# A long-convolution layer with a relu MLP on one core: the product stage regrouped by four frequencies, with a shifted tile for one of its results

## Chip, core, metric

One core of one Trainium2 chip runs the whole program. The metric is device microseconds (us) of one execution. Three executions of the kernel before took 213.0, 213.03 and 213.28 us, so the median is 213.03 us. All other times come from one further execution that was recorded by the hardware profiler: it took 213.07 us in all, of which 211.2 us are the span from the first recorded instruction to the last.

The engines are TensorE (PE for its matmuls, PEld for its weight loads), VectorE (DVE), ScalarE (ACT), GpSimd (POOL) and SyncE (SP, which only issues DMAs). L425 means line 425 of the kernel before.

## What is computed

Input x, k and v are 2048 tokens of 512 channels. The reference, cut to what matters:

```python
k_shift = short causal convolution of k over 4 tokens
kv   = k_shift * v
y    = irfft(rfft(kv padded to 4096) * rfft(ssm_k padded to 4096))[:2048]
h    = x + layernorm(x) * (y + kv * ssm_D)
out  = h + relu(layernorm(h) @ w1) @ w2          # w1 is 512 x 1376, w2 is 1376 x 512
```

The transform, the product and the inverse transform are done as matmuls with tables of sines, in 4-byte floats.

## The kernel before, in words

**Stages.** (1) Up to about 51 us: loads, sine tables, the short convolution (`taps`, L333), transposes of its input (`to_rows`, L278) and the first half of the forward transform (`stage1`, L294) of the filter into the tile BK and of the data into the tile BX. (2) 51.1 to 91.1 us: **the product stage** (L418 to L455), the second half of both forward transforms, frequency index k1 = 0 to 31, and the product of filter and data. (3) 91.1 to 114.2 us: the first half of the inverse transform (`inv1`, L541), 16 blocks. (4) to the end: the second half of the inverse (`inv2`, L634), the gate, and the MLP.

**The product stage.** BK and BX have the places [2 parts i][32 g][32][8] in each of 128 partitions. For one k1, `cols` takes the g of one parity, k1 % 2, and there the two places 2v and 2v+1 with v = k1 // 2: the data of k1 = 2v and of k1 = 2v+1 lie in the same two places, one in the even g and the other in the odd g. Two kinds of unit work on them; each unit has a PSUM buffer of two banks and runs an x = 0 part on BK and then an x = 1 part on BX:

- `pairs(k1)` (tile u, L425): 8 matmuls of 64 rows by 256 columns, which run two at a time, one on the upper and one on the lower 64 rows of the array. That makes 4 steps of two matmuls each: parts i = 0 and i = 1 on BK, then i = 0 and i = 1 on BX. Its product is written in place into `BK[:, :, :, k1, :]`, that is, into place k1 of every g, odd and even.
- `sums(k1)` (tile us, L435): 8 matmuls of 128 rows by 256 columns, for k1 and k1 + 1, with weights from the table tile smc. Its product is written in place into `BX[:, 0, :, k1:k1+2, :]`.

A step below is the start-to-start time of such matmuls. `times` (L439) then finishes a unit: ACT copies the BK half of the PSUM buffer to SBUF (`forms`, L415, tiles ktu and kts with two buffers each), and DVE multiplies it with the other half and writes the product (L442).

The order is written out by hand: for every two k1 the loop (L445) issues the matmuls of `sums(k1)`, `pairs(k1)`, `pairs(k1 + 1)`, and then `times` of the three. ACT and DVE take units in that same order. For k1 = 0 all x = 0 parts come first. The pool psF has four buffers of two banks, so a unit may start only when the product of the fourth unit before it has been read out by DVE. The semaphore waits follow from the order of issue and from what overlaps: a product waits for all matmuls issued before it that read the places it overwrites.

`sum_tables(c)` (L376) lets POOL write the weights for the sums of four k1 into one of four places of smc; the first four groups are made before the stage, the others follow as places come free. `add_chunks` (L406, POOL) prepares column sums of w1, which `column_means` (L460, tile pm) needs right after the stage.

**After it.** `inv1_mm` (L535) makes one output of 256 columns from three accumulated matmuls: part 0 on the sums' products (`BX[:, 0]`, with inv3), parts 1 and 2 on the two halves of the pairs' products (BK, with inv12). All three are 256 columns wide; in parts 1 and 2 half of the 256 columns of the table are zeros. `inv1_begin` starts part 0 of blocks 0 and 1. Everything contracts over all k1, so no inverse matmul can run before the last products that it reads are written.

Of the kernel before, what the change touches and what calls it, by code (L numbers as in the profile page):

```python
# [10 lines left out]
BF16 = mybir.dt.bfloat16  # L11
F32 = mybir.dt.float32
F32R = mybir.dt.float32r
I32 = mybir.dt.int32
PSUM = bass.MemoryType.PSUM
P = 128
# [40 lines left out]
def kernel(  # L57
# [13 lines left out]
    nc = tc.nc  # L71
# [5 lines left out]
    DC = D // P  # L77
    NFC = (DFF + P - 1) // P
    x_d, k_d, v_d, out_d = A_q[0], A_k[0], A_v[0], out[0]
    lo, hi = slice(0, 64), slice(64, 128)  # L80
    halves = (lo, hi)

    pl = _Pools(tc)
    ctx.enter_context(tc.manual_schedule())
    consts = pl.push("consts")
    bkp = pl.push("bkp")
    bxp = pl.push("bxp")
    c0p = pl.push("c0p")
    stp = pl.push("stp")
    skp = pl.push("skp")  # L90
    early = pl.push("early")
    xkp = pl.push("xkp", side="right")
    psum = pl.push("psF", bufs=4, space=PSUM)

    BK = bkp.tile([P, 2, 32, 32, DC * 2], F32R, tag="K", name="BK")
    E = bxp.tile([P, 16384], F32, tag="X", name="E")
    F = xkp.tile([P, 4096], F32, tag="F", name="F")
    G = skp.tile([P, 4096], I32, tag="G", name="G")  # L100
    taken = [15424]

    def view(at, n, dt, t=E):
# [22 lines left out]
    for dp in range(2):  # L126
        src = bass.AP(tensor=A_ssm_D.tensor, offset=A_ssm_D.offset, ap=[[0, 1], [1, DC * P]])
        nc.scalar.dma_start(out=draw[64 * dp:64 * dp + 1, :], in_=src)
    zero = consts.tile([P, 512], BF16, name="zero")
    nc.vector.memset(zero[:], 0.0)  # L130
    nc.vector.memset(kT[0][:, :, 0:16], 0.0)
    for c in range(4):
# [20 lines left out]
    def fill(ps, n):  # L153

        for _ in range(n):
            nc.tensor.matmul(out=ps, lhsT=zero[:, 0:P], rhs=zero[:], start=True, stop=True, skip_group_check=True)

    fill(bank2("psz")[:, 0, :], 22)

# [46 lines left out]
    dpm = small([2, 64], F32)  # L206
# [10 lines left out]
    st = stp.tile([P, 32, 192], F32R, name="st")  # L217
# [12 lines left out]
    for dp in range(2):  # L230
        row = slice(64 * dp, 64 * dp + 1)
        for rp in range(2):
            for sp in range(2):
                src = draw[row, 256 * rp:256 * rp + 256].rearrange("p (r u s l d) -> p r u s l d", r=2, s=2, l=2, d=2)[:, :, :, sp, :, dp]
# [8 lines left out]
    esc = consts.tile([P, DC], F32, name="esc")  # L243
    ebi = consts.tile([P, DC], F32, name="ebi")
    core0 = c0p.tile([P, 32, P], F32R, name="core0")
    ecore = [core0[:].rearrange("p (h i r) x -> p h i r x", h=2, i=4)] + [None] * 3
    ecw = {0: tsn.rearrange("p a b -> p (a b)")[:, 0:1024].rearrange("p (h x) -> p h x", h=2)}

    def ec_turns(q):
# [9 lines left out]

    def ec_sins(q, rs=range(DC)):  # L260
        for r in rs:
            nc.scalar.activation(out=ecore[q][:, :, :, r, :], in_=ecw[q].rearrange("p h (i x) -> p h i x", i=4),  # L262
                                 func=ACT.Sin, scale=esc[:, r:r + 1], bias=ebi[:, r:r + 1])

    def copy(eng, o, i):
# [72 lines left out]


    inv3 = consts.tile([P, 2, 2, 64], F32R, name="inv3")  # L340
    inv12 = consts.tile([P, 6, 64], F32R, name="inv12")
    ones = consts.tile([P, P], F32R, name="ones")
    for gb in range(7):
        if gb == 6:
# [13 lines left out]
            taps(gb // 2, gb % 2)  # L358

    nc.gpsimd.memset(inv3[:].bitcast(F32), 0.0)  # L360
    nc.gpsimd.memset(inv12[:].bitcast(F32), 0.0)
    nc.gpsimd.tensor_tensor(out=dpm[:, 0, :], in0=dsc[:, 0, :], in1=dsc[:, 1, :], op=ALU.add)
    nc.gpsimd.tensor_tensor(out=dpm[:, 1, :], in0=dsc[:, 1, :], in1=dsc[:, 0, :], op=ALU.subtract)
    for dst, pq, src, sgn in ((inv12[lo, 2, :], lo, dpm[lo, 0, :], 1.0), (inv12[lo, 3, :], lo, dpm[lo, 1, :], 1.0),
                              (inv12[hi, 2, :], hi, dpm[hi, 1, :], 1.0), (inv12[hi, 3, :], hi, dpm[hi, 0, :], -1.0),
                              (inv3[lo, 0, 0, :], lo, dsc[lo, 1, :], -1.0), (inv3[lo, 0, 1, :], lo, dsc[lo, 0, :], 1.0),
                              (inv3[hi, 1, 0, :], hi, dsc[hi, 1, :], -1.0), (inv3[hi, 1, 1, :], hi, dsc[hi, 0, :], 1.0)):
        nc.gpsimd.tensor_single_scalar(out=dst, in_=src, scalar=sgn / 2048, op=ALU.mult)
    nc.gpsimd.memset(ones[:].bitcast(F32), 1.0 / D)


    smc = skp.tile([P, 4, 2, 4, P], F32R, tag="G", name="smc")
    for dp, pq in enumerate(halves):
        nc.gpsimd.memset(smc[pq, :, :, :, 64 - 64 * dp:128 - 64 * dp].bitcast(F32), 0.0)

    def sum_tables(c):  # L376
        ks = slice(4 * c, 4 * c + 4)
        for dp, pq in enumerate(halves):
            for i, op in ((0, ALU.subtract), (1, ALU.add)):
                nc.gpsimd.tensor_tensor(out=smc[pq, c % 4, i, :, 64 * dp:64 * dp + 64], in0=st[pq, ks, 64:128].bitcast(F32),  # L380
                                        in1=st[pq, ks, 0:64].bitcast(F32), op=op)

    for c in range(4):
        sum_tables(c)

    xfl = xkp.tile([P, P, 64], BF16, tag="F", name="xfl")
    for h in range(4):
        to_rows(vT, h, xfl[:])
    stage1(kfl, BK, 7, dmask)
    BX = bxp.tile([P, 2, 32, 32, DC * 2], F32R, tag="X", name="BX")  # L390
    for gb in range(8):
        stage1(xfl, BX, gb)
    pl.pop("xkp")
# [12 lines left out]
    def add_chunks(step):  # L406
        o, a, b = ((wsum, w1[:, 0, :], w1[:, 1, :]), (wpair, w1[:, 2, :], w1[:, 3, :]), (wsum, wsum.bitcast(F32), wpair.bitcast(F32)))[step]
        nc.gpsimd.tensor_tensor(out=o, in0=a, in1=b, op=ALU.add)
# [9 lines left out]
    def pairs(k1):  # L418

        ps = bank2("u")  # L420

        def do(x):
            for i, t in ((0, st[:, k1, 64:192]), (1, st[:, k1, 0:128])):
                for dp, pq in enumerate(halves):
                    nc.tensor.matmul(out=ps[:, dp, 256 * x:256 * x + 256], lhsT=t[pq], rhs=cols((BK, BX)[x], pq, k1, i),  # L425
                                     start=(i == 0), stop=(i == 1), tile_position=(64 * dp, 0), skip_group_check=True)
        return do, ps, "ktu", BK[:, :, :, k1, :]

    def sums(k1):
        ps = bank2("us")  # L430

        def do(x):
            for k in (k1, k1 + 1):
                for i in range(2):
                    nc.tensor.matmul(out=ps[:, k % 2, 256 * x:256 * x + 256], lhsT=smc[:, k // 4 % 4, i, k % 4, :],  # L435
                                     rhs=cols((BK, BX)[x], slice(0, P), k, i), start=(i == 0), stop=(i == 1), skip_group_check=True)
        return do, ps, "kts", BX[:, 0, :, k1:k1 + 2, :].rearrange("p g k x -> p k g x")

    def times(unit):  # L439
        do, ps, tag, o = unit  # L440
        kt = forms(ps[:, :, 0:256], tag)
        nc.vector.tensor_tensor(out=o, in0=ps[:, :, 256:512].rearrange("p b (g x) -> p b g x", x=8),  # L442
                                in1=kt[:].rearrange("p b (g x) -> p b g x", x=8), op=ALU.mult)

    for k1 in range(0, 32, 2):  # L445
        units = [sums(k1), pairs(k1), pairs(k1 + 1)]

        for n, x in sorted(((n, x) for n in range(3) for x in range(2)), key=lambda nx: nx[::-1] if k1 == 0 else nx):
            units[n][0](x)
        for unit in units:  # L450
            times(unit)
        if k1 % 4 == 2 and k1 // 4 + 4 < 8:
            sum_tables(k1 // 4 + 4)
        if k1 in (18, 20, 22):
            add_chunks((k1 - 18) // 2)  # L455

    FS = 344
    cen = {}
# [25 lines left out]
    st = late.tile([P, 4, 6], F32, name="st")  # L484
# [3 lines left out]
    rstd2 = late.tile([P, NT, 1], F32, name="rstd2")  # L488
    mhalf = late.tile([P, 4], F32, name="mhalf")
    for q in (1, 2):  # L490
        ecore[q] = BX[:, 0, 16 * q - 16:16 * q].rearrange("p g c x -> p (g c x)").rearrange("p (h i r x) -> p h i r x", h=2, i=4, r=DC)
    ecore[3] = ecore[0]
    xT = [late.tile([P, 4, DC, P], BF16, name="xT0")[:]] + [None] * 3
    qT = [late.tile([P, 4, DC, P], BF16, name="qT0")[:]] + [None] * 3
# [33 lines left out]
                                in1=cen[n].unsqueeze(1).to_broadcast([P, DC, FS]), op=ALU.subtract)  # L528

    ax1 = late.tile([P, 32, 2, P], F32R, name="ax1")  # L530
    ax = (BX[:, 1].rearrange("p g c x -> p (g c x)").rearrange("p (n m c) -> p n m c", m=2, c=P), ax1[:])

    blocks = {}

    def inv1_mm(b, i, parts, i0=0):  # L535
        g = 4 * b + i0 + i
        o = blocks[b][:, i].rearrange("p d a n -> p (d a n)")
        for part in parts:
            src = BX[:, 0] if part == 0 else BK[:, part - 1]
            rhs = inv3[:].rearrange("p d a n -> p (d a n)") if part == 0 else inv12[:, 4 - 2 * part:8 - 2 * part, :].rearrange("p a n -> p (a n)")  # L540
            nc.tensor.matmul(out=o, lhsT=src[:, g // 2, :, g % 2::2].rearrange("p c r -> p (c r)"), rhs=rhs,  # L541
                             start=(part == 0), stop=(part == 2), skip_group_check=True)

    def inv1_begin(b):

# [80 lines left out]
    def inv2(q, pool):  # L626
        pz = pool.tile([P, 4, DC, 4, 32], F32, tag="pz", name="pz")
        pzs[q] = pz
        for j in range(16):
            i, a = j // 4, j % 4  # L630
            w = min(2, 4 - a)
            n2 = 16 * a + 4 * q + i
            for rho in range(2):
                nc.tensor.matmul(out=pz[:, i, :, a:a + w, :].rearrange("p r a n -> p r (a n)"),  # L634
                                 lhsT=ax[rho][:, n2 // 2, n2 % 2, :],
                                 rhs=ecore[q][:, rho, i, :, 32 * a:32 * a + 32 * w],
                                 start=(rho == 0), stop=(rho == 1), skip_group_check=True)

    def mlp1(sc, hook=None):
# [106 lines left out]
```

## Time and profile before

| | us |
|---|---|
| median of three executions | 213.03 |
| the profiled execution, in all | 213.07 |
| its span | 211.2 |
| busy PE, DVE, ACT, POOL | 201.9, 141.4, 116.1, 70.4 |
| product stage, 51.1 to 89.1: PE, DVE, ACT, POOL busy of 38.0 | 38.0, 29.6, 26.8, 20.2 |
| 89.1 to 91.1: PE, DVE busy of 2.0 | 1.7, 1.9 |
| first half of the inverse, 91.1 to 114.2: PE, DVE, ACT busy of 23.1 | 23.1, 16.4, 17.1 |
| granted TensorE clock in all of these | 1.00 |

The first rows say that about 2 us of an execution lie outside of the span; a difference in the span is read as the same difference in the time. The stage rows come from the view that sums each engine's busy time over stretches of the span. An engine that is busy for a whole stretch is not necessarily at its best there: the PE rows count a matmul from its start to the modelled end of its result, so that steps overlap. The chain of waits (the work that ended last, followed backward) tells which engine sets the time in each stage; the timeline tells the start of single groups of instructions.

### The profile page before, as it was taken

The page shows a single profiled execution, that of the slowest core. Times are in us where ns is not written, and L with a number is a line of the kernel's source. Part 1 is how long each engine was busy: PE and PEld are TensorE (multiplying, and loading weights), DVE is VectorE, ACT ScalarE, POOL GpSimd, SP SyncE. Part 2 cuts the span into 40 slices and gives each one's busy share as a digit, 9 for nine tenths or more (in the row PEclk, how much of TensorE's full clock was granted, in tenths as well). Part 3 has the DMA queues.
Part 4 walks back from the last instruction along what each step waited for, and adds up shares of the span by engine and source line. Part 5 has one row for each costly group of instructions (what it writes and reads, how often), then busy time and mean ns, then how long its engine had stood idle before and what let it go on. Part 6 is the DMA issues. An engine that isn't in the chain of part 4 may idle for free.

```text
span 211.2 us, 4330 instructions
## 1 busy us (share of the span) xinstructions
PE 201.9 (96%) x1735; PEld 138.5 (66%) x1735; DVE 141.4 (67%) x244; ACT 116.1 (55%) x188; POOL 70.4 (33%) x119
## 2 busy tenths in 40 slices
PE   7889999989999999999999999999999999999991
PEld 2475555977888888889998954448444844444451
DVE  5978987699678887899445487896278833252131
ACT  3987776687677677757593039501970066017300
POOL 7954704995555893030203020620202010002000
PEclk9999999999999999999999999999999999999999
DMA  5999970000700000038224998999906615110011
GB/s 147 350 209 183 226 95 2 3 5 15 255 3 0 3 0 3 0 99 102 45 55 111 273 210 168 136 166 133 172 4 126 144 27 96 31 52 22 0 50 50
DMA packets 47818, 19.91 MB, mean 94 GB/s; under 512 B 42710, under 2 KB 46264, under 8 KB 47800
## 3 DMA queue, kind: packets, MB, share of 16 engines
q1 hardware_dynamic: 44144, 16.15, 42.1%
q10 hardware_dynamic: 3656, 3.51, 6.1%
q8 instruction: 13, 0.21, 0.4%
q14 instruction: 5, 0.04, 0.1%
HBM read 7.02 MB, written 2.10 MB: 43 GB/s over the span
## 4 chain that ended last, share of the span: by engine, by line
PE 84%; DVE 5%; DMA 4%; ACT 4%; issue 1%; SPq 0%; DVEq 0%
PE ps2m L662 18%; PE ps1m L646 14%; PE psi L541 11%; PE u L425 9%; PE us L435 9%; PE ps L294 8%; PE pkv L333 7%; PE pz L634 5%; DMA E<-in_A_ssm_k_dram 4%; PE pst L278 3%; ACT BX L262 2%; DVE st L499 1%; ACT M L648 1%; DVE qT L620 1%; ACT xfl L281 0%
## 5 line engine op out<-in xcount | busy, mean ns | idle before, releaser
L648 ACT ACTIVATE M<-ps1m 128x512 bf16<-128x512 f32 (+1 forms) x44 | 25.0, 602 | 50.0 <-PE ps1m L646 39.5
L662 PE MATMUL ps2m<-M 128*128 128x512 bf16 (+3 forms) x187 | 38.8, 366 | 0.0
L662 PEld LDWEIGHTS <-M 128*128 128x128 bf16 (+1 forms) x187 | 18.2, 98 | 20.0 <-ACT M L648 0.4
L646 PEld LDWEIGHTS <-w 128*128 128x128 bf16 (+1 forms) x176 | 17.4, 100 | 20.5 <-issue 0.9
L380 POOL TENSOR_TENSOR smc<-st 64x256 fp32r<-64x256 f32 x32 | 22.8, 732 | 11.1 <-PE us L435 10.2
L503 POOL TENSOR_SCALAR rstd<-mv 128x4 f32<-128x4 f32 x8 | 2.2, 277 | 71.0 <-DVE mv L501 71.0
L664 DVE SCALAR_TENSOR_TENSOR M<-ps2m,rstd,M 128x512 bf16<-128x512 f32 (+1 forms) x13 | 9.2, 708 | 24.3 <-PE ps2m L662 15.7
L541 PE MATMUL psi<-inv,BK 128*128 128x256 f32 x128 | 22.7, 282 | 0.0
L442 DVE TENSOR_TENSOR BK<-u,ktu 128x512 fp32r<-128x512 f32 x32 | 20.4, 680 | 0.0
L541 PEld LDWEIGHTS psi<-inv,BK 128*128 128x128 f32 x128 | 19.9, 195 | 0.0
L646 PE MATMUL ps1m<-xT,w 128*128 128x512 bf16 (+1 forms) x88 | 19.6, 379 | 0.3 <-ACT M L648 0.2
L646 PE MATMUL ps1m<-M,w 128*128 128x512 bf16 (+1 forms) x88 | 19.3, 379 | 0.0
L541 PE MATMUL psi<-inv,BX 128*128 128x256 f32 x64 | 18.0, 286 | 0.1
L415 ACT COPY ktu<-u 128x512 f32<-128x512 f32 x32 | 17.2, 589 | 1.5
L442 DVE TENSOR_TENSOR BX<-us,kts 128x512 fp32r<-128x512 f32 x16 | 11.1, 692 | 8.4 <-PE u L425 6.8
L415 ACT COPY kts<-us 128x512 f32<-128x512 f32 x16 | 9.4, 588 | 9.6 <-PE us L435 9.6
L425 PE MATMUL u<-BK,st 64*128 64x256 f32 x128 | 14.6, 308 | 0.0
L499 DVE BATCH_NORM_STATS2 st<-M 128x6 f32<-128x512 bf16 x20 | 12.3, 677 | 1.1 <-DMA M<-M 1.1
L425 PE MATMUL u<-BX,st 64*128 64x256 f32 x128 | 13.0, 284 | 0.0
L309 ACT CAST BK<-ps 128x512 fp32r<-128x512 f32 x16 | 9.4, 586 | 6.1 <-PE ps L294 4.0
L541 PEld LDWEIGHTS psi<-inv,BX 128*128 128x128 f32 x64 | 12.3, 195 | 0.6 <-DVE BK L442 0.6
L435 PE MATMUL us<-BK,smc 128*128 128x256 f32 x64 | 12.0, 310 | 0.0
(127 smaller groups left out, 401.8 us busy)
## 6 DMA issues: line engine op xcount, KB each, us to landing
E<-in_A_ssm_k_dram SPq DMA_DIRECT2D x1, 2048.0 KB
out_dram<-M ACTq DMA_DIRECT2D x15, 128.0 KB
w<-in_B_w_dram SPq DMA_DIRECT2D x1, 1376.0 KB
M<-in_B_w_dram ACTq DMA_DIRECT2D x1, 1280.0 KB
M<-in_A_q_dram SPq DMA_DIRECT2D x8, 128.0 KB
xh<-in_A_q_dram SPq DMA_DIRECT2D x4, 128.0 KB
xr<-in_A_q_dram SPq DMA_DIRECT2D x4, 128.0 KB
out_dram<-M ACTq DMA_DIRECT2D x2, 64.0 KB
```

The lines of the kernel that those rows point to most:

```text
L294: nc.tensor.matmul(out=pss[rp][:, gi // 2, :, gi % 2, :], lhsT=fl[rows, 2 * g:2 * g + 2, :].rearrange("p d n -> p (d n)"), rhs=f[rows].rea ...
L333: nc.tensor.matmul(out=ps[:, i, :], lhsT=wdiag[:, 2 * h + i, j, :], rhs=kT[c][:, 2 * h + i, 16 - j:CH + 16 - j], start=(j == 0), stop=(j = ...
L380: nc.gpsimd.tensor_tensor(out=smc[pq, c % 4, i, :, 64 * dp:64 * dp + 64], in0=st[pq, ks, 64:128].bitcast(F32), in1=st[pq, ks, 0:64].bitcas ...
L415: nc.scalar.copy(out=kt[:], in_=ps)
L425: nc.tensor.matmul(out=ps[:, dp, 256 * x:256 * x + 256], lhsT=t[pq], rhs=cols((BK, BX)[x], pq, k1, i), start=(i == 0), stop=(i == 1), tile ...
L435: nc.tensor.matmul(out=ps[:, k % 2, 256 * x:256 * x + 256], lhsT=smc[:, k // 4 % 4, i, k % 4, :], rhs=cols((BK, BX)[x], slice(0, P), k, i) ...
L442: nc.vector.tensor_tensor(out=o, in0=ps[:, :, 256:512].rearrange("p b (g x) -> p b g x", x=8), in1=kt[:].rearrange("p b (g x) -> p b g x", ...
L499: nc.vector.bn_stats(out=st[:, i, :], in_=src[:, i, :])
L541: nc.tensor.matmul(out=o, lhsT=src[:, g // 2, :, g % 2::2].rearrange("p c r -> p (c r)"), rhs=rhs, start=(part == 0), stop=(part == 2), sk ...
L646: nc.tensor.matmul(out=ps1[:fsz, :].rearrange("p (i t) -> p i t", i=4), lhsT=w1[:, c, fc * P:fc * P + fsz], rhs=hT[sc][:, :, c, :], start= ...
L648: nc.scalar.activation(out=h1T[:fsz, fc, :], in_=ps1[:fsz, :], func=ACT.Relu)
L662: nc.tensor.matmul(out=ps2, lhsT=h1T[:ksz, fc, i * P:(i + 1) * P], rhs=w2[:ksz, fc, d0:d0 + w], start=(fc == 0), stop=(fc == NFC - 1))
```

## The change

Four things change together.

1. **The order.** The loop runs over c = 0 to 7, four k1 each: `pairs(4c)`, `sums(4c)`, `sums(4c + 2)`, `pairs(4c + 1)`, then, between two calls of `times`, `pairs(4c + 2)` and `pairs(4c + 3)`. ACT and DVE finish the units in the order in which the array runs them.
2. **The tile.** BX gets 66 places instead of 64 per g. The data lie in places 2 to 65; the sums' products go to places 0 to 31 (`BXs`), so that the product for k1 lands on the data (i = 0) of k1 - 2 and k1 - 1. All readers of the sums' products and of the tile's later uses (`ecore`, `ax`, `inv1_mm`) get the new view.
3. **Room for it.** smc has three places instead of four; the zero tile for the opening matmuls is 128 instead of 512 wide and read four times over; inv12 loses its zeros, so parts 1 and 2 of `inv1_mm` write 128 columns each, into the first and the second half of the output.
4. **Pools** are opened and closed at other places and sides, with the same tiles sharing memory one after the other.

```diff
-    smc = skp.tile([P, 4, 2, 4, P], F32R, tag="G", name="smc")
+    pl.pop("turnp")
+    skp = pl.push("skp")
+    smc = skp.tile([P, 3, 2, 4, P], F32R, name="smc")
...
-    for c in range(4):
+    for c in range(3):
         sum_tables(c)
...
-    BX = bxp.tile([P, 2, 32, 32, DC * 2], F32R, tag="X", name="BX")
+
+    BXt = bxp.tile([P, 32, 66, DC * 2], F32R, tag="X", name="BX")
+    BX = BXt[:, :, 2:66, :].rearrange("p g (i k) x -> p i g k x", i=2)
+    BXs = BXt[:, :, 0:32, :]
...
-        return do, ps, "kts", BX[:, 0, :, k1:k1 + 2, :].rearrange("p g k x -> p k g x")
+        return do, ps, "kts", BXs[:, :, k1:k1 + 2, :].rearrange("p g k x -> p k g x")
...
-    for k1 in range(0, 32, 2):
-        units = [sums(k1), pairs(k1), pairs(k1 + 1)]
-
-        for n, x in sorted(((n, x) for n in range(3) for x in range(2)), key=lambda nx: nx[::-1] if k1 == 0 else nx):
+
+    for c in range(8):
+        units = [pairs(4 * c), sums(4 * c), sums(4 * c + 2), pairs(4 * c + 1)]
+
+        for n, x in sorted(((n, x) for n in range(4) for x in range(2)), key=lambda nx: nx[::-1] if c == 0 else nx):
             units[n][0](x)
+        for k1 in (4 * c + 2, 4 * c + 3):
+            times(units.pop(0))
+            units.append(pairs(k1))
+            for x in range(2):
+                units[-1][0](x)
         for unit in units:
             times(unit)
-        if k1 % 4 == 2 and k1 // 4 + 4 < 8:
-            sum_tables(k1 // 4 + 4)
-        if k1 in (18, 20, 22):
-            add_chunks((k1 - 18) // 2)
+        if c + 3 < 8:
+            sum_tables(c + 3)
+        if c in (4, 5, 6):
+            add_chunks(c - 4)
...
-            src = BX[:, 0] if part == 0 else BK[:, part - 1]
-            rhs = inv3[:].rearrange("p d a n -> p (d a n)") if part == 0 else inv12[:, 4 - 2 * part:8 - 2 * part, :].rearrange("p a n -> p (a n)")
-            nc.tensor.matmul(out=o, lhsT=src[:, g // 2, :, g % 2::2].rearrange("p c r -> p (c r)"), rhs=rhs,
-                             start=(part == 0), stop=(part == 2), skip_group_check=True)
+            src = BXs if part == 0 else BK[:, part - 1]
+            rhs = inv3[:].rearrange("p d a n -> p (d a n)") if part == 0 else inv12[:].rearrange("p a n -> p (a n)")
+            nc.tensor.matmul(out=o if part == 0 else o[:, P * part - P:P * part], lhsT=src[:, g // 2, :, g % 2::2].rearrange("p c r -> p (c r)"), rhs=rhs,
+                             start=(part == 0), stop=(part > 0), skip_group_check=True)
```

More of the change, by code (lines that the diff above doesn't have):

```diff
@@ L89 @@
     stp = pl.push("stp")
-    skp = pl.push("skp")
-    early = pl.push("early")
-    xkp = pl.push("xkp", side="right")
+    turnp = pl.push("turnp")
+    early = pl.push("early", side="right")
+    kp = pl.push("kp", side="right")
     psum = pl.push("psF", bufs=4, space=PSUM)
     BK = bkp.tile([P, 2, 32, 32, DC * 2], F32R, tag="K", name="BK")
-    E = bxp.tile([P, 16384], F32, tag="X", name="E")
-    F = xkp.tile([P, 4096], F32, tag="F", name="F")
-    G = skp.tile([P, 4096], I32, tag="G", name="G")
+    E = bxp.tile([P, 16896], F32, tag="X", name="E")
+    F = kp.tile([P, 2112], F32, name="F")
+    G = turnp.tile([P, 4096], I32, name="G")
     taken = [15424]
@@ L128 @@
         nc.scalar.dma_start(out=draw[64 * dp:64 * dp + 1, :], in_=src)
-    zero = consts.tile([P, 512], BF16, name="zero")
+    zero = consts.tile([P, P], BF16, name="zero")
     nc.vector.memset(zero[:], 0.0)
@@ L155, in fill @@
         for _ in range(n):
-            nc.tensor.matmul(out=ps, lhsT=zero[:, 0:P], rhs=zero[:], start=True, stop=True, skip_group_check=True)
+            nc.tensor.matmul(out=ps, lhsT=zero[:], rhs=zero[:].unsqueeze(1).to_broadcast([P, 4, P]), start=True, stop=True, skip_group_check=True)
     fill(bank2("psz")[:, 0, :], 22)
@@ L245 @@
     core0 = c0p.tile([P, 32, P], F32R, name="core0")
-    ecore = [core0[:].rearrange("p (h i r) x -> p h i r x", h=2, i=4)] + [None] * 3
+    ecore = [core0[:].rearrange("p (h i s r) x -> p h i s r x", h=2, i=4, s=2)] + [None] * 3
     ecw = {0: tsn.rearrange("p a b -> p (a b)")[:, 0:1024].rearrange("p (h x) -> p h x", h=2)}
@@ L261, in ec_sins @@
         for r in rs:
-            nc.scalar.activation(out=ecore[q][:, :, :, r, :], in_=ecw[q].rearrange("p h (i x) -> p h i x", i=4),
+            nc.scalar.activation(out=ecore[q][:, :, :, r // 2, r % 2, :], in_=ecw[q].rearrange("p h (i x) -> p h i x", i=4),
                                  func=ACT.Sin, scale=esc[:, r:r + 1], bias=ebi[:, r:r + 1])
@@ L340 @@
     inv3 = consts.tile([P, 2, 2, 64], F32R, name="inv3")
-    inv12 = consts.tile([P, 6, 64], F32R, name="inv12")
+    inv12 = consts.tile([P, 2, 64], F32R, name="inv12")
     ones = consts.tile([P, P], F32R, name="ones")
@@ L360 @@
     nc.gpsimd.memset(inv3[:].bitcast(F32), 0.0)
-    nc.gpsimd.memset(inv12[:].bitcast(F32), 0.0)
     nc.gpsimd.tensor_tensor(out=dpm[:, 0, :], in0=dsc[:, 0, :], in1=dsc[:, 1, :], op=ALU.add)
     nc.gpsimd.tensor_tensor(out=dpm[:, 1, :], in0=dsc[:, 1, :], in1=dsc[:, 0, :], op=ALU.subtract)
-    for dst, pq, src, sgn in ((inv12[lo, 2, :], lo, dpm[lo, 0, :], 1.0), (inv12[lo, 3, :], lo, dpm[lo, 1, :], 1.0),
-                              (inv12[hi, 2, :], hi, dpm[hi, 1, :], 1.0), (inv12[hi, 3, :], hi, dpm[hi, 0, :], -1.0),
+    for dst, pq, src, sgn in ((inv12[lo, 0, :], lo, dpm[lo, 0, :], 1.0), (inv12[lo, 1, :], lo, dpm[lo, 1, :], 1.0),
+                              (inv12[hi, 0, :], hi, dpm[hi, 1, :], 1.0), (inv12[hi, 1, :], hi, dpm[hi, 0, :], -1.0),
                               (inv3[lo, 0, 0, :], lo, dsc[lo, 1, :], -1.0), (inv3[lo, 0, 1, :], lo, dsc[lo, 0, :], 1.0),
@@ L379, in sum_tables @@
             for i, op in ((0, ALU.subtract), (1, ALU.add)):
-                nc.gpsimd.tensor_tensor(out=smc[pq, c % 4, i, :, 64 * dp:64 * dp + 64], in0=st[pq, ks, 64:128].bitcast(F32),
+                nc.gpsimd.tensor_tensor(out=smc[pq, c % 3, i, :, 64 * dp:64 * dp + 64], in0=st[pq, ks, 64:128].bitcast(F32),
                                         in1=st[pq, ks, 0:64].bitcast(F32), op=op)
-    for c in range(4):
+    for c in range(3):
         sum_tables(c)
-    xfl = xkp.tile([P, P, 64], BF16, tag="F", name="xfl")
+    pl.pop("kp")
+    xkp = pl.push("xkp", side="right")
+    xfl = xkp.tile([P, P, 64], BF16, name="xfl")
     for h in range(4):
@@ L434, in do @@
                 for i in range(2):
-                    nc.tensor.matmul(out=ps[:, k % 2, 256 * x:256 * x + 256], lhsT=smc[:, k // 4 % 4, i, k % 4, :],
+                    nc.tensor.matmul(out=ps[:, k % 2, 256 * x:256 * x + 256], lhsT=smc[:, k // 4 % 3, i, k % 4, :],
                                      rhs=cols((BK, BX)[x], slice(0, P), k, i), start=(i == 0), stop=(i == 1), skip_group_check=True)
-        return do, ps, "kts", BX[:, 0, :, k1:k1 + 2, :].rearrange("p g k x -> p k g x")
+        return do, ps, "kts", BXs[:, :, k1:k1 + 2, :].rearrange("p g k x -> p k g x")
     def times(unit):
@@ L490 @@
     for q in (1, 2):
-        ecore[q] = BX[:, 0, 16 * q - 16:16 * q].rearrange("p g c x -> p (g c x)").rearrange("p (h i r x) -> p h i r x", h=2, i=4, r=DC)
+        ecore[q] = BXs[:, 16 * q - 16:16 * q].rearrange("p (h i s) k x -> p h i s (k x)", h=2, i=4).rearrange("p h i s (r x) -> p h i s r x", r=2)
     ecore[3] = ecore[0]
@@ L530 @@
     ax1 = late.tile([P, 32, 2, P], F32R, name="ax1")
-    ax = (BX[:, 1].rearrange("p g c x -> p (g c x)").rearrange("p (n m c) -> p n m c", m=2, c=P), ax1[:])
+    ax = (BX[:, 1].rearrange("p n k x -> p n (k x)").rearrange("p n (m c) -> p n m c", m=2), ax1[:])
     blocks = {}
@@ L633, in inv2 @@
             for rho in range(2):
-                nc.tensor.matmul(out=pz[:, i, :, a:a + w, :].rearrange("p r a n -> p r (a n)"),
+                nc.tensor.matmul(out=pz[:, i, :, a:a + w, :].rearrange("p (s r) a n -> p s r (a n)", s=2),
                                  lhsT=ax[rho][:, n2 // 2, n2 % 2, :],
-                                 rhs=ecore[q][:, rho, i, :, 32 * a:32 * a + 32 * w],
+                                 rhs=ecore[q][:, rho, i, :, :, 32 * a:32 * a + 32 * w],
                                  start=(rho == 0), stop=(rho == 1), skip_group_check=True)
```

## The prediction

> **What bounds the kernel now.** I read the chain of waits first: which engine sets the end, stage by stage.
>
> ```profile
> PE 84%; DVE 5%; DMA 4%; ACT 4%; issue 1%; SPq 0%; DVEq 0%
> ...
> 86.85 1.17 PE us L435 x8
> 88.01 1.06 PE u L425 x14
> 89.08 0.03 issue
> 89.10 0.02 DVEq L442
> 89.12 0.04 issue
> 89.17 0.69 DVE BX L442
> ```
>
> In the product stage the chain never leaves PE: 1.17 us for a sums unit, 1.17 for two pairs units, over and over. Only when the last matmul is done does it go to DVE. So inside the stage PE's own pace counts, and at its end DVE's last products. The timeline of PE alone shows that pace (one two-k1 block, and the start of the next):
>
> ```profile
> 65.77 0.75 PE L435 MATMUL us<-BK,smc 128*128 128x256 f32 x4
> 66.37 0.65 PE L435 MATMUL us<-BX,smc 128*128 128x256 f32 x4
> 66.94 0.51 PE L425 MATMUL u<-BK,st 64*128 64x256 f32 x4
> 67.29 0.41 PE L425 MATMUL u<-BX,st 64*128 64x256 f32 x4
> 67.54 0.41 PE L425 MATMUL u<-BK,st 64*128 64x256 f32 x4
> 67.78 0.40 PE L425 MATMUL u<-BX,st 64*128 64x256 f32 x4
> 68.11 0.39 PE L435 MATMUL us<-BK,smc 128*128 128x256 f32 x1
> ```
>
> Inside a kind, two steps of pairs take 67.54 to 67.78, 0.12 us a step. Eight steps would be 0.96, but sums to pairs is 66.94 - 65.77 = 1.17: each change between 128-row and 64-row matmuls costs 0.21. A block of 2.34 us is 16 x 0.12 + 2 x 0.21. Last, the timeline of all engines at the stage's end, for the latencies:
>
> ```profile
> 88.77 0.41 PE L425 MATMUL u<-BX,st 64*128 64x256 f32 x4
> 89.11 0.30 PEld L464 LDWEIGHTS pm<-st,ones 128*128 128x128 f32 x2
> ...
> 89.17 0.69 DVE L442 TENSOR_TENSOR BX<-us,kts 128x512 fp32r<-128x512 f32 x1 [0.45 <-PE u L425]
> 89.78 1.28 DVE L442 TENSOR_TENSOR BK<-u,ktu 128x512 fp32r<-128x512 f32 x2
> 89.91 0.30 PEld L464 LDWEIGHTS pm<-st,ones 128*128 128x128 f32 x2 [0.51 <-DVE BX L442]
> ```
>
> The sums' product waits for the i = 0 step on BX of the last pairs unit (start 88.77) and begins at 89.17: **0.39** from a releasing step to DVE. Products follow each other every **0.605** (89.17, 89.78, and 1.28 for two of 0.68) and each is complete after **0.69** (sums) or **0.68** (pairs). From 89.86 to 89.91, **0.05**, PE's next weight load starts; a first step after such a wait needs **0.11** more for its load.
>
> **Part 1, the order: fewer changes of kind.** Per four k1, before: 32 steps x 0.12 + 4 x 0.21 = 4.68 (trace: 2 x 2.337 = 4.67). After, the array runs p0 s0 s2 p1 p2 p3 (p for pairs, s for sums): two changes, 3.84 + 0.42 = 4.26. Gain 0.42 per group, if nothing waits.
>
> **Part 2, what now waits.** Something does. p2 is the fourth unit after p0, so it needs p0's PSUM buffer, hence p0's finished product. That product overwrites place 4c of every g in BK; the odd g there hold data of k1 = 4c + 1, which p1 still reads (its columns are places 4c and 4c + 1 of the odd g). The matmuls of p1 are issued before the product, so the product waits for p1's BK steps; the instructions as built carry both waits. Before, the products waited as long, but the fourth buffer let PE run on: the unit that needed the first product came 1.17 us of sums later. Now the next unit is the one that waits, and behind the first product DVE has two sums' products queued. With m the start of p1's last BK step:
>
> - p0's product starts m + 0.39, ends m + 1.07; p2's load m + 1.12, its first step m + 1.23. Unhindered it is m + 0.36 (three steps). **Stall 0.87.**
> - p3 needs s0's product: start m + 0.995, end m + 1.685, PE's step m + 1.85. p2's four steps end m + 1.71. **Stall 0.14.**
> - the next p0 needs s2's product: start m + 1.60, end m + 2.29, step m + 2.45, against 1.85 + 0.48 = 2.33. **Stall 0.13.** (s2's own wait, p1's i = 0 step on BX, clears earlier.)
>
> Later units wait for nothing: p1's product is complete at m + 2.89, and the next s0 loads after p0's four steps and a change, m + 3.02. The group thus takes 4.26 + 1.14 = 5.40 against 4.67: **+0.72**. Bounds for the three stalls together, from the rows: if each waiting op saw its release as fast as ACT does (88.74 for a step of 88.41, so 0.33 and not 0.39), 1.08; if each of three event waits in the chain cost 0.05 more (the handover seen above), 1.29. I take 1.14.
>
> **Part 3, first group and last.** With all x = 0 parts first, p1's reads are over before p0's product is due, and the stall is gone; the array makes 4 changes as before. Adding the steps, changes and the wait for the last stage1 buffer (ACT's copy ends 52.21), then 0.27 for s0's product and 0.12 for s2's, I get 5.25 from 51.13 to the next group, against 5.29 in the trace: -0.04. In the last group PE needs 4.26 + 0.87 + 0.14 = 5.27; the change to the column means makes it 5.36 until their load. The tail after that: ktu has two buffers, so ACT's copy of p3 waits for p1's product (m + 2.89) and DVE ends at m + 4.25, the second inverse block loads at m + 4.30, 1.88 after the load of the column means (before: 89.11 to 91.11, 2.00). Group and tail 7.24 against 6.67: **+0.57**. Sum of the stage: 6 x 0.72 + 0.57 - 0.04 = **+4.85**.
>
> **Part 4, inverse parts of 128 columns.** 128 matmuls (L541) halve. The chain gives 23.08 us for 190 there, 0.12 each, the same 0.12 as wherever weights are 4-byte. What 128 columns cost is in `inv2`:
>
> ```profile
> 115.79 0.28 PE L634 MATMUL pz<-core,ax 128*128 128x256 f32 x1
> 115.90 0.22 PE L634 MATMUL pz<-core,BX 128*128 128x128 f32 x1
> 115.96 0.28 PE L634 MATMUL pz<-core,ax 128*128 128x128 f32 x1
> 116.07 0.34 PE L634 MATMUL pz<-core,BX 128*128 128x256 f32 x1
> 116.25 0.28 PE L634 MATMUL pz<-core,ax 128*128 128x256 f32 x1
> 116.36 0.28 PE L634 MATMUL pz<-core,BX 128*128 128x256 f32 x1
> ```
>
> 115.90 to 116.36 is 0.46 for two of 128 and two of 256 columns: less 2 x 0.12, a step of 128 costs 0.11. The transposes (L278, 128 columns, weights with a stride) go at 9 more per 1.00 us, 0.111. I read that as the load of the weights, which is as long for both. The inverse's strided loads are a little longer (195 ns against 188 in `inv2`), so I take 0.113: 128 x 0.007 = **-0.9**; ends 0.004 (-0.5) and 0.010 (-1.3).
>
> Against this stands a rule. The Trainium skill, "TensorE: Matmul & The Clock Gate", section Back-to-back issue gap, puts the isolated gap at N / 2.4 + 2.5 ns, which is 56 ns at 128 columns and 109 at 256. By it an estimate is 128 x 0.053 = 6.8 us saved, more than the stage loses, and a time of about 211.2. The rows of 0.11 are of the same chip and kind of data, so the rule is not in my sum.
>
> **Part 5, the rest.** stage1's copies into BX get one dimension more. DVE is back to back there (eight copies, about 1.22 each, and PE waits for them), so an increase is paid; the nearest pair of rows for a dimension more is 680 against 692 ns: 8 x 0.012 = **+0.1**, between 0 and that, no gain. The ring of three tables is covered: POOL makes one in 4 x 0.73 = 2.9 us, more than 10 us ahead of use; the cover gone, each would cost up to 2.9. add_chunks (2.82 + 2.82 + 3.16) would end near 87, the column means need them near 94. The memset that goes (inv12), the smaller zero tile and the pools' places lie on POOL and DVE where they set nothing. No DMA is added, and SP's order is the same.
>
> **Sum.** 4.85 - 0.9 + 0.1 = +4.05 on the profiled 213.07: **217.1 us**. The median before, 213.03, is the same within 0.04.
>
> **Rivals.**
> - *The cover holds* (faster): p0's product doesn't have to wait for p1, and p2 finds its buffer free. Then 7 x -0.42, a shorter tail of -0.3, -0.04, -0.9 + 0.1, in all -4.1: 209.0. For it: DVE is idle 6.8 us before sums' products in waits that the shifted tile takes away. Against: that tile only frees sums' products; p0's is of BK. It decides from 0.7 us less per group. 0.10.
> - *Weight loads don't bind*: the inverse gains several us, until ACT's two copies a block bind; 211 to 213. Against it the 0.11 rows. 0.04.
> - *Only the first stall is real*, p3 and the next p0 being just covered: 6 x 0.45 + 0.43 - 0.04 - 0.8 = +2.3, 215.4. 0.16.
> - *Stalls run longer*: DVE's event waits take time between products, 0.25 more in each of seven groups: 218.9. 0.10.
> - Forecast: 0.60. Its own range is 216.2 to 218.4: six groups at the stalls' bounds (-0.06 and +0.15 each), the ends of part 4, and part 5 at nothing. Not done as told? The built order on PE is p s s p p p, so that is excluded.
>
> **Numbers.** The range takes in the third rival and the fourth: 215.0 to 219.0. That leaves out the two fast cases, 0.14. About 0.2% (0.4 us) is what a measurement can tell from no change: slower 0.86, same 0.02, faster 0.12.
>
> **What would show it.** In the trace after: pairs to p2 with an idle of 0.8 to 0.9 us on PE in seven groups, released by DVE's product into BK; groups of 5.4 us from c = 1; DVE in runs of six products with a pause of about 1.5; psi near 22.2 us in place of 23.1; changes of kind halved. Wrong if p2 follows p1 without idle time, or if psi's steps of 128 columns start 0.06 apart.

## The result and the profile after

The changed kernel takes **217.8 us** (217.67 to 217.9, four executions) against 213.07 us for the kernel before on the same chip: a ratio of 1.022, 95% interval 1.0202 to 1.0238. It is slower, as forecast (217.1, range 215.0 to 219.0). The profiled execution took 217.9 us with a span of 216.0. Some executions of several of these kernels take about 1.4 us more at a lower granted clock (in the trace of e5 below it is 0.84 between 9 and 20 us, against 1.00 there in the trace after), so that a median of few executions is read beside the trace.

The chain of waits by engine, from the page of the kernel after, and two lines of the view of waits (engine and line that waits, who ends it; total us, times, longest):

```profile
PE 79%; DMA 7%; DVE 6%; ACT 4%; issue 1%; SPq 0%; DVEq 0%; ACTq 0%
```

```profile
PEld u L431 <- DVE BK L448: 5.8, 7, 0.8
PE u L431 <- DVE BK L448: 4.3, 7, 0.6
```

PE has gone from 84% to 79% of the chain and DVE from 5% to 6%, which is what the second fence explains: seven times, once in each group but the first, the array waits for a product into BK. The weight loads' row (0.8 each) is nearer to what the wait costs than the matmuls' row (0.6), because a matmul is counted as busy to the modelled end of its result. (In the kernel after, L431 is `pairs`, L441 `sums`, L421 `forms`, L448 `times` and L553 `inv1_mm`.) The DMA's new 7% is no new cost: from the end of the inverse's first half to DVE's next statistics (st) it is 8.40 us after (118.88 to 127.28) and 8.38 before (114.19 to 122.57); only the wait that is named last has changed.

One group of the chain after, in order of time (start, us, what):

```profile
65.27 0.70 DVE BK L448
65.97 0.04 issue
66.01 1.94 PE u L431 x24
67.96 2.12 PE us L441 x16
70.08 0.45 PE u L431 x4
70.53 0.03 issue
70.56 0.02 DVEq L448
```

Before, the stage had no DVE line until the last matmul. Now each group goes through one: p1's BK steps (70.08), DVE's product, then 24 matmuls of p2, p3 and the next p0 and 16 of the two sums. The timeline of all engines around the first DVE piece of that fence (start, us; what ended the idle time in brackets):

```profile
64.64 0.51 PE L431 MATMUL u<-BK,st 64*128 64x256 f32 x4
...
64.99 0.40 PE L431 MATMUL u<-BX,st 64*128 64x256 f32 x4
65.27 0.69 DVE L448 TENSOR_TENSOR BK<-u,ktu 128x512 fp32r<-128x512 f32 x1 [1.51 <-PE u L431]
...
65.87 1.28 DVE L448 TENSOR_TENSOR BX<-us,kts 128x512 fp32r<-128x512 f32 x2
66.01 0.51 PE L431 MATMUL u<-BK,st 64*128 64x256 f32 x4 [0.62 <-DVE BK L448]
66.36 0.41 PE L431 MATMUL u<-BX,st 64*128 64x256 f32 x4
66.61 0.50 PE L431 MATMUL u<-BK,st 64*128 64x256 f32 x4
...
67.07 1.28 DVE L448 TENSOR_TENSOR BK<-u,ktu 128x512 fp32r<-128x512 f32 x2
67.21 0.51 PE L431 MATMUL u<-BK,st 64*128 64x256 f32 x4
```

At 64.64 p1 loads; its first step of BX starts at 64.99, so its last BK step, 0.12 before, starts at 64.87. DVE begins p0's product 0.40 later, it is complete at 65.96, and p2 loads at 66.01. p3 (66.61) and the next p0 (67.21) each come 0.60 after the unit before them, where four steps are 0.48: they follow DVE's pace of one product in 0.60. Groups are 5.38 us apart.

The stage's end and the inverse, from the chain:

```profile
96.09 22.79 PE psi L553 x190
```

Before it was 23.08. From the first load of the product stage to the load of the second inverse block it is 45.00 us after (51.09 to 96.09) and 39.98 before (51.13 to 91.11): +5.02. The inverse gives back 0.29, and the rest of the span differs by less than 0.1 in sum: 216.0 - 211.2 = 4.8.

### The profile page after: what moved, and what is told of

It reads as the page before. It is cut to its first block, busy times and chain, and to the rows that moved or that the text cites. A ratio compares the mean times of both kernels' runs of the same rounds, so it can differ in the third digit from the quotient of the medians.

```text
span 216.0 us, 4337 instructions
## 1 busy us (share of the span) xinstructions
PE 201.3 (93%) x1735; PEld 138.5 (64%) x1735; DVE 140.7 (65%) x244; ACT 117.6 (54%) x188; POOL 70.0 (32%) x118
## 4 chain that ended last, share of the span: by engine, by line
PE 79%; DMA 7%; DVE 6%; ACT 4%; issue 1%; SPq 0%; DVEq 0%; ACTq 0%
PE ps2m L674 18%; PE ps1m L658 14%; PE psi L553 11%; PE u L431 8%; PE us L441 8%; PE ps L294 8%; PE pkv L333 7%; DMA E<-in_A_ssm_k_dram 4%; DMA M<-in_B_w_dram 4%; PE pz L646 3%; PE pst L278 3%; DVE BK L448 3%; ACT BX L262 2%; DVE st L511 1%; ACT M L660 1%
## 5 line engine op out<-in xcount | busy, mean ns | idle before, releaser
L448 DVE TENSOR_TENSOR BK<-u,ktu 128x512 fp32r<-128x512 f32 x32 | 21.3, 686 | 13.3 <-PE u L431 10.4
L421 ACT COPY ktu<-u 128x512 f32<-128x512 f32 x32 | 18.7, 587 | 11.4 <-PE u L431 7.1
L553 PE MATMUL psi<-inv,BX 128*128 128x256 f32 x64 | 21.5, 341 | 0.3 <-DVE BK L448 0.3
L553 PE MATMUL psi<-inv,BK 128*128 128x128 f32 x128 | 21.5, 254 | 0.0
L431 PE MATMUL u<-BK,st 64*128 64x256 f32 x128 | 16.3, 333 | 4.3 <-DVE BK L448 4.3
L553 PEld LDWEIGHTS psi<-inv,BK 128*128 128x128 f32 x128 | 20.0, 197 | 0.0
L431 PEld LDWEIGHTS u<-BK,st 64*128 64x128 f32 x128 | 9.5, 184 | 7.9 <-DVE BK L448 5.8
L431 PE MATMUL u<-BX,st 64*128 64x256 f32 x128 | 13.1, 283 | 0.0
L553 PEld LDWEIGHTS psi<-inv,BX 128*128 128x128 f32 x64 | 12.4, 196 | 0.8 <-DVE BK L448 0.8
L337 DVE TENSOR_TENSOR E<-pkv,E 128x1024 bf16<-128x1024 f32 (+1 forms) x9 | 9.9, 1105 | 2.7 <-PE pkv L333 2.7
L421 ACT COPY kts<-us 128x512 f32<-128x512 f32 x16 | 9.3, 587 | 3.7 <-PE us L441 2.9
```

Of the source, the lines that this page charges most:

```text
L421: nc.scalar.copy(out=kt[:], in_=ps)
L553: nc.tensor.matmul(out=o if part == 0 else o[:, P * part - P:P * part], lhsT=src[:, g // 2, :, g % 2::2].rearrange("p c r -> p (c r)"), rh ...
```

## Experiments

Two explanations of the loss stand against each other. Mine: the array waits for a buffer whose product must wait for p1, so the place of p1 in the order costs the time. The rivals: the new tile, the ring of three (smc's three places) or DVE's load cost it.

### e1: p1 ahead of the sums

```diff
-        units = [pairs(4 * c), sums(4 * c), sums(4 * c + 2), pairs(4 * c + 1)]
+        units = [pairs(4 * c), pairs(4 * c + 1), sums(4 * c), sums(4 * c + 2)]
```

> The changed kernel with one edit: the second pairs unit is moved ahead of the two sums units, p0 p1 s0 s2 p2 p3. Tile, ring of three, narrow inverse tables and the number of changes of kind (two per group) stay. My theory (p2 waits for p0's product, which waits for p1's BK reads): p0's product now waits for s0's BK steps only and is complete before p2 comes; by the same latencies a group takes 4.28 us instead of 5.39, the last tail is about 0.3 shorter, so about 217.8 - 7 x 1.1 - 0.3 = 209.8 us, and PE has no idle time on DVE's product into BK. Rival 1 (the ring of three tables, or the shifted tile's strides, hold the groups up): 217 to 218, groups still above 5. Rival 2 (DVE's six products a group, 3.6 us, are the bound together with their waits): groups between 4.7 and 5.1, 213 to 216.

Measured: 210.64 us, ratio to the kernel before 0.9896 (0.9864 to 0.9928). Groups are 4.36 us apart. From the chain of e1:

```profile
62.13 2.19 PE us L441 x16
64.32 2.17 PE u L431 x32
66.49 0.02 issue
66.52 2.18 PE us L441 x16
```

A group is one run of sums and one run of pairs again, 2.19 + 2.17, with no DVE piece between them. Neither rival survives: ring, strides and the six products of DVE are all still there. It is 0.8 us slower than I expected; 0.08 of that comes in each group. The timeline shows a short wait of the array in front of s0:

```profile
72.91 1.48 DVE L448 TENSOR_TENSOR BX<-us,kts 128x512 fp32r<-128x512 f32 x2
...
73.31 0.42 PE L431 MATMUL u<-BX,st 64*128 64x256 f32 x4
...
73.77 1.08 ACT L421 COPY ktu<-u 128x512 f32<-128x512 f32 x2
...
74.39 1.29 DVE L448 TENSOR_TENSOR BK<-u,ktu 128x512 fp32r<-128x512 f32 x2
...
75.20 0.30 PEld L441 LDWEIGHTS us<-BK,smc 128*128 128x128 f32 x2 [0.22 <-issue]
```

The next s0 needs p2's buffer. p2's last matmuls end at 73.73, ACT's copy of p2 runs from 73.77 to 74.36, DVE's product from 74.39 to 75.08, and s0 loads at 75.20. This way through ACT and DVE is about 0.1 us longer than the twelve steps and the change of kind that PE has in between. DVE itself isn't full: the 1.48 of the two sums' products, against 1.29 for two pairs' products, holds a pause in front of s2's until ACT's copy of s2 is done (73.66). The profile names no releaser for s0's load, so that p2's product ends this wait is read from the times alone: in all six such groups the load comes 0.12 after it. The first group also took about 5.6 us instead of 5.25, since its third unit comes sooner and meets stage1's last copy out of PSUM (it ends at 52.02 in this trace).

### e2: the old order in the new tile

The loop of the kernel before stands in the changed kernel, with `sum_tables(k1 // 4 + 3)` for the ring of three.

> The changed kernel with the old order of units (s0 p0 p1 for every two k1, four changes of kind in four k1); shifted tile, ring of three and narrow inverse tables stay. My theory: everything but the order is nearly free, so two k1 take 2.337 us as before; the sums' product doesn't wait for the pairs any more, which shortens the last tail by 0.4, and the narrow tables give 0.3: about 212.4 us. Rival (tile, ring or pools cost time by themselves): 213.1 or more, two k1 above 2.35 us.

Measured: 212.5 us, ratio 0.9992 (0.997 to 1.0014), by itself not distinguishable from no change. The trace tells more. From its chain:

```profile
86.72 1.17 PE us L441 x8
87.89 0.70 PE u L431 x8
...
90.57 22.77 PE psi L548 x190
```

Blocks of two k1 are 2.33 us, and from the load of the column means (88.98) to the second inverse block (90.57) it is 1.59 instead of 2.00: the shorter tail of 0.4 is there, since sums' products no longer wait for pairs, and so is the inverse's 0.3. The span is 210.5, 0.7 below the kernel before, which is these two gains. With the old order, tile, ring and pools cost nothing.

### e3: narrow inverse tables alone

```diff
-    inv12 = consts.tile([P, 6, 64], F32R, name="inv12")
+    inv12 = consts.tile([P, 2, 64], F32R, name="inv12")
...
-                             start=(part == 0), stop=(part == 2), skip_group_check=True)
+                             start=(part == 0), stop=(part > 0), skip_group_check=True)
```

> The kernel before with one part of the change: inverse tables without zeros, so that 128 of the 192 matmuls of the inverse's first half write 128 columns instead of 256. From the trace after, where 190 of them took 22.79 us instead of 23.08: 212.8 us, and a step of 0.118 to 0.119. My forecast had 0.9 for this part: 212.1. Rival (the gain in the trace after comes from elsewhere): 213.1.

Measured: 212.58 us, ratio 0.9982 (0.9967 to 0.9998); the 190 matmuls take 22.73 us in its chain, against 23.08. The part is worth 0.3 to 0.4, and not the 0.9 of the prediction.

### e4: sums first

```diff
-        units = [pairs(4 * c), sums(4 * c), sums(4 * c + 2), pairs(4 * c + 1)]
+        units = [sums(4 * c), sums(4 * c + 2), pairs(4 * c), pairs(4 * c + 1)]
```

> The changed kernel with both sums units first: s0 s2 p0 p1 p2 p3, two changes of kind per group as in the other orders. My theory: p2 now needs s0's buffer, which is free; but p3 needs s2's, and s2's product overwrites X data that p1 still reads, so it starts 0.39 after p1's third step and p3 stalls about 0.5. Group 4.76 us, between 4.28 and 5.39: about 217.8 - 7 x 0.63 = 213.4 us, with PE idle in front of p3 on DVE's product into BX, not into BK. Rival 1 (ring of three or strides): 217 to 218. Rival 2 (fewer changes of kind are all that counts): 4.3 a group, 209.9.

Measured: 213.55 us, ratio 1.0029 (1.0007 to 1.005); groups of 4.78. The timeline of e4, around p3:

```profile
69.28 0.69 DVE L448 TENSOR_TENSOR BX<-us,kts 128x512 fp32r<-128x512 f32 x1 [0.77 <-PE u L431]
...
69.88 1.28 DVE L448 TENSOR_TENSOR BK<-u,ktu 128x512 fp32r<-128x512 f32 x2
70.02 0.51 PE L431 MATMUL u<-BK,st 64*128 64x256 f32 x4 [0.25 <-DVE BX L448]
```

The wait has moved as it should: the array now idles in front of p3, and it is DVE's product into BX (s2's) that ends it. Three orders with the same number of changes of kind (e1, e4, the changed kernel) give 4.36, 4.78 and 5.38 us; they differ in which product a unit has to wait for.

### e5: the wait taken away, nothing moved

```diff
-                    nc.tensor.matmul(out=ps[:, dp, 256 * x:256 * x + 256], lhsT=t[pq], rhs=cols((BK, BX)[x], pq, k1, i),
+                    nc.tensor.matmul(out=ps[:, dp, 256 * x:256 * x + 256], lhsT=t[pq], rhs=cols((BK, BX)[x], pq, k1 + 2 * (k1 % 4 == 1), i),
```

> The changed kernel with its own order p0 s0 s2 p1 p2 p3 on every engine; only p1 reads the columns of k1 = 4c + 3 in place of those of 4c + 1 (so a quarter of the pairs' products is computed from other data and the output isn't the reference's). Same work, same order, but what p0's product overwrites is not read by p1 any more, nor what s2's product overwrites. My theory: the stall goes without any move; a group takes 4.28 to 4.36 us, the tail stays as in the changed kernel: about 217.8 - 6 x 1.06 - 1.0 = 210.4 us. Rival (putting the sums side by side is what costs, through the order of buffers or DVE's load): 217 to 218, groups of 5.4.

Measured: a median of 211.9 us (ratio 0.9923, 0.9894 to 0.9952); the shortest of six executions took 210.42. What decides is the length of the groups. From the chain:

```profile
62.86 2.17 PE us L441 x16
65.03 2.15 PE u L431 x32
67.18 0.03 issue
67.21 2.17 PE us L441 x16
```

Groups are 4.35 us, with the order of the changed kernel on every engine. Only the data that p1 reads is other data, so that products may overwrite their places sooner. That shows it directly: the order by itself is harmless; the overlap of p0's and s2's targets with p1's columns costs the 1.0 us per group. e5 frees both products at once; that p0's is the one that counts first is seen in the trace after, where p2 waits for a product into BK.

### e6 and e7: the inverse with packed weights

```diff
-            nc.tensor.matmul(out=o if part == 0 else o[:, P * part - P:P * part], lhsT=src[:, g // 2, :, g % 2::2].rearrange("p c r -> p (c r)"), rhs=rhs,
+            nc.tensor.matmul(out=o if part == 0 else o[:, P * part - P:P * part], lhsT=src[:, g // 2, 16 * (g % 2):16 * (g % 2) + 16, :].rearrange("p c r -> p (c r)"), rhs=rhs,
```

e6 is this edit in the changed kernel, e7 the same weights in the kernel before.

> The changed kernel with packed weights in the inverse's first half: each matmul loads 128 neighbouring values in place of every second one (other data, so the output isn't the reference's). In the trace after, a cycle of 256, 128 and 128 columns takes 0.355 us, 0.118 a step, though 128 columns cost 0.11 in the second half of the inverse, whose weights are packed. My theory: the stride of the loads is the difference; steps behind 128 columns go to 0.109, the cycle to 0.337, so 64 x 0.018 = 1.2 us less: 216.6, psi 21.6 us long. Rival (128 columns into one half of a bank, or the accumulation, cost it): 217.8, psi 22.8.

> The kernel before (256 columns in all three parts) with the same packed weights, output not the reference's. My theory: behind 256 columns a step is 0.119 to 0.120 with packed weights too, as in the second half of the inverse: 213.0, psi 23.0 us long. Rival (the load sets the pace here as well): steps of 0.11, psi 21.2, time 211.2.

Measured: e6 216.75 us, ratio 1.019 (1.0159 to 1.0222), where the changed kernel stands at 1.022; e7 213.11, ratio 1.0021 (1.0001 to 1.004). The inverse's lines of the two chains, e6 first:

```profile
95.88 21.82 PE psi L553 x190
```

```profile
91.15 23.07 PE psi L541 x190
```

And the steps, in the kernel after and then in e6:

```profile
98.40 0.34 PE L553 MATMUL psi<-inv,BX 128*128 128x256 f32 x1
98.57 0.34 PE L553 MATMUL psi<-inv,BK 128*128 128x128 f32 x2
98.76 0.34 PE L553 MATMUL psi<-inv,BX 128*128 128x256 f32 x1
```

```profile
100.14 0.33 PE L553 MATMUL psi<-inv,BX 128*128 128x256 f32 x1
100.31 0.34 PE L553 MATMUL psi<-inv,BK 128*128 128x128 f32 x2
100.48 0.33 PE L553 MATMUL psi<-inv,BX 128*128 128x256 f32 x1
```

A cycle of three (one matmul of 256 columns, two of 128) takes about 0.356 us with the stride and 0.34 without. With 256 columns in all three parts packing changes nothing (23.07 against 23.08); with two parts of 128 it is worth 1.0 us in all (I expected 1.2). So it is the stride of the weights that held the narrow matmuls up. If the 256 columns take 0.12 of a cycle, as they do in e7, the rest is 0.118 a step with the stride and 0.11 without, an estimate.

### e8: the good order without the new tile

The kernel before, with e1's loop and `sum_tables(c + 4)`.

> The kernel before, with only the order that removed the stall (p0 p1 s0 s2 p2 p3 by four k1): no shifted tile, sums' products in place, four tables, wide inverse tables. My theory: two changes of kind per group, but s2's product now overwrites X data that p2 and p3 still read, so it starts 0.39 after p3's third step; the next p1, which needs its buffer, stalls 0.5. Group 4.76 against 4.67 before: about 213.0 + 7 x 0.09 = 213.6 us, PE idle in front of p1 on DVE's product into BX. Rival (the order alone does it and the tile was not needed): groups of 4.36, 210.9 us.

Measured: 214.1 us, ratio 1.0047 (1.003 to 1.0064), groups of 4.80. Its timeline:

```profile
66.19 0.69 DVE L442 TENSOR_TENSOR BX<-us,kts 128x512 fp32r<-128x512 f32 x1 [0.62 <-PE u L425]
...
66.93 0.51 PE L425 MATMUL u<-BK,st 64*128 64x256 f32 x4 [0.24 <-DVE BX L442]
```

In place, s2's product must wait for p3, and the next p1 waits for s2's buffer. e1's order gains only with the shifted tile: without it, it is slower than the kernel before. I expected 213.6; 0.04 more in each group and the first group's wait for stage1's last copy, as in e1, are most of the difference.

## Why the prediction was right, point by point

- **The stalls** were right in mechanism and size. Forecast: p0's product 0.39 after p1's last BK step, p2 held up by 0.87, p3 by 0.14, the next p0 by 0.13, groups of 5.40. Trace: 0.40, p2's first step 1.14 + 0.11 after that step instead of 0.36 (0.89), 0.12 each for the other two, groups of 5.38. e4 and e5 show that these are the waits that cost, each with its own unit.
- **The changes of kind** at 0.21 were right: without the stalls the group falls to 4.36 and 4.35 (e1, e5), against 4.67 with four changes; the 0.42 that two changes save, less about 0.1 of remaining waits.
- **First and last group** were near: 5.36 to the next group's first load instead of 5.25, and 7.38 instead of 7.24 to the second inverse block. Of the latter 0.11 is an error of adding up: p1's last BK step is 3.05 after the group's first load, which with m + 4.30 makes 7.35; the 7.24 begins at p0's first step, 0.11 after its load. The stage as a whole: +5.02, forecast +4.85.
- **The inverse's narrow parts** were mis-sized: the step that failed is "I take 0.113" for a step of 128 columns. That figure leaned on packed weights in `inv2` and on a wider stride in the transposes. With this stride (every second value) a step takes about 0.118, so 0.29 us came instead of 0.9, outside the ends of 0.5 to 1.3. e3 (0.35 in the chain) and e6 confirm it. This one term is most of the 0.7 us between 217.1 and 217.8. By the isolated gap of the Trainium skill, "TensorE: Matmul & The Clock Gate", section Back-to-back issue gap, an estimate had been 6.8 us; the section itself says that this gap under-counts at small N because it has no weight loads in it, and the runs show 0.3, about a twentieth.
- **stage1's copies** cost nothing more: the eight on DVE have a median of 1220 ns in both traces, so +0.1 was 0.
- **Rivals.** "The cover holds" priced the kernel without the stalls at 209.0. e1 at 210.64 comes near that kernel; the remaining waits, its longer first group and the smaller gain of the inverse lie between. "Only the first stall is real" falls with the 0.12 that p3 and the next p0 wait in each group, "stalls run longer" with groups of 5.38, and "weight loads don't bind" with steps of 0.118.

The version that beats both is e1: the changed kernel with p1 issued ahead of the sums, 0.9896 of the kernel before and 7.2 us below the changed kernel. Its remaining wait of about 0.1 us a group was not worked on.

## What to carry to other kernels

When the order of issue is regrouped so that a costly switch is paid less often, write down for every unit which buffer it reuses, which result frees that buffer, and what that result must wait for before it may overwrite its target; here a move of one unit by two places was worth 7 us, more than twice what the regrouping could bring. Here two units that share storage (p0 and p1) belong side by side in the order. And the saving on streamed columns was only as large as the gap to the next limit, the load of the weights, which has to be measured with the same stride.

## What the runs showed of the hardware

- Matmuls of 128 columns, each with its own load of 128 by 128 weights of 4 bytes, follow each other at about 0.118 us when the load takes every second value (kernel after) and at about 0.11 when the weights are packed (e6), both worked out of cycles of three; with 256 columns the step is 0.12 in both cases (kernel before, e7).
- A change between matmuls on 128 rows and on two halves of 64 rows costs about 0.21 us beyond the 0.12 of a step (1.17 for eight steps and a change in the trace before). With two changes in four k1 a group takes 4.36 us (e1, with 0.1 of waits in it), with four 2 x 2.33 (e2).
